# Moving part of one query tile's feed-forward work out of the tail, five instead of six shared head groups before it, and a later due slot for side work

## The chip, the cores and the metric

One NeuronCore of a Trainium2 chip runs one transformer block. The metric is the time of one execution in device microseconds (us). TensorE is called PE here, VectorE is DVE, ScalarE is ACT. "The trace" is the record that the hardware profiler makes of one execution.

Before the change the kernel took 922.74 us (median of 3 runs, 921.8 to 923.44).

## The reference, cut

```python
def _A_ref(x, wqkv, wo):            # B, S, D = 1, 2048, 512; H = 32 heads of 16
    qkv = (x @ wqkv).reshape(B, S, 3, H, Dh).transpose(2, 0, 3, 1, 4)
    scores = jnp.einsum('bhqd,bhkd->bhqk', q, k) * Dh ** (-0.5)
    p = _softmax(scores, axis=-1)
    o = jnp.einsum('bhqk,bhkd->bhqd', p, v)
    return o.transpose(0, 2, 1, 3).reshape(B, S, D) @ wo

def _B_ref(x, w_gate, w_up, w_down):        # F = 1792
    return _gelu(x @ w_gate) * (x @ w_up) @ w_down

h = _layernorm(x) * (1 + ca) + sa           # sa .. gb: six rows of silu(c) @ w_mod
x = x + ga * _A_ref(h, A_wqkv, A_wo)
h = _layernorm(x) * (1 + cb) + sb
x = x + gb * _B_ref(h, B_w_gate, B_w_up, B_w_down)
```

The softmax has 32 x 2048 x 2048 exponentials. On 128 partitions that is 2048 slices of 512 columns.

## The kernel before: the parts that matter

The 2048 queries are worked off in six sets. The last two are single tiles of 128 queries; I call them A (tile 14) and B (tile 15). Heads come in eight "quads" of four heads. For the first six quads, A and B run as one unit of 256 queries; for the last two quads each runs alone, A first.

```python
SETS = ((0, 512), (512, 512), (1024, 512), (1536, 256), (1792, 128), (1920, 128))
QS = 6              # quads in which A and B share a unit
LATE = 48
...
units += [((4, 5), qd, SETS[4][0], 2 * P) for qd in range(QS)]
units += [((k,), qd) + SETS[k] for k in (4, 5) for qd in range(QS, 8)]
```

A "slot" is one slice of 512 score columns. ACT exponentiates most of them, two or three slots in one instruction. Where DVE has room, one slot of three is given to DVE instead, which needs five instructions for it.

Beside the attention of one set, PE works off "side work" of the sets before: output projection, LayerNorm, and the feed-forward block (gate, up, down), all through one PSUM bank. Each piece has a start slot and a due slot, and is spread evenly between them:

```python
due = (ends[1] + 30, ends[2] + 30, ends[3] + 30, n - LATE)    # feed-forward of sets 0..3
...                                                           # then, for A (k):
w.append((lambda: self.near_end(k, 6, self.mi[:, 0:P]), s0, s0))      # normalisers of its
w.append((lambda: self.near_end(k, 7, self.mi[:, 0:P]), s0, s0))      # last two quads
w.append((lambda: self.side_wo(k), s0, s0))                           # output projection
w.append((self.scale_wo, s0, s0))
w.append((lambda: self.near_end(k + 1, 6, self.mi[:, 0:P]), s0, s0))  # B's quad 6
```

What is left when the last exponential is done is the tail. It interleaves A's feed-forward block (14 blocks of 128 hidden columns in four chunks of 4, 4, 4 and 2: 112 gate and up matmuls and 14 down matmuls) with B's whole end: last PV round, normaliser of quad 7, output projection, LayerNorm, and the same feed-forward block.

```python
def tail_end(self, k):                       # B
    ...                                      # normaliser of quad 7, output projection into bank
    self.task([lambda: self.ln_stat(tile, bank)] + self.ln2_steps(k, bank), ("ln2", k))
    self.task([("act", lambda: self.act(self.xs[:, tile, :], bank, ACT.Copy))], ("x1", k))
    yield from self.until(("ln2", k))
    for h in range(2):
        pb = self.scp[:, 4 + h, :]
        yield lambda h=h, pb=pb: self.transp(pb, lambda t: self.normed(k, t), 1, h)
        for i in range(2):
            dc = 2 * h + i
            self.modulate("act" if i == 0 else "dve", self.t2T[:, dc, c0:c0 + W], ...)
    yield from self.tail_ffn(k, self.mi[:, :], (4, 5, 0, 1, 2, 3), 4)
```

The softmax here doesn't subtract the row's maximum and nothing guards it: scores larger than these inputs give would overflow.

## Time and profile before

| | before |
|---|---|
| time | 922.74 us |
| span of the profiled execution | 919.5 us, granted PE clock 0.999 |
| ACT busy | 890.8 us (97%) |
| last exponential ends | 892.92 us |
| from there to the end ("the tail") | 26.56 us |

From the page of the kernel before: span and busy times by engine.

```profile
span 919.5 us, 17368 instructions
PE 779.0 (85%) x7222; PEld 259.7 (28%) x7342; DVE 759.8 (83%) x1482; ACT 890.8 (97%) x749; POOL 3.6 (0%) x11
```

The groups of ACT instructions, shapes kept apart, of the kernel before: the columns after the bar are busy time in us and mean ns of one, then idle time just before them and its cause.

```profile
L309 ACT ACTIVATE E<-ps_sc 128x1536 bf16<-128x1536 f32 x510 | 736.4, 1614 | 1.9 <-PE ps_sc L296 1.9
L309 ACT ACTIVATE E<-ps_sc 128x1024 bf16<-128x1024 f32 x182 | 211.3, 1181 | 0.4 <-PE ps_sc L296 0.4
```

ACT waits for scores only 2.3 us in the whole run. A slice less in an instruction is worth 1614 - 1181 = 433 ns.

The chain that ended last, the kernel before, from the last exponentials on (start, length, what; steps called `issue`, 0.05 us or less, are left out here and below):

```profile
879.47 13.43 ACT E L309 x10
892.92 1.28 ACT L309
...
895.22 0.34 DVE wreg L321
895.56 0.88 DVE rb L333
896.46 0.30 DVE onorm L313
896.81 3.52 PE ps_sc L296 x57
...
914.78 0.70 DVE xw L313
...
916.76 0.42 DVE xs L313
```

Read it from the top. The last exponential ends, ACT loads the table for gelu (1.28 us), DVE modulates tile A (`wreg`) and only then takes the reciprocal of B's last normaliser (`rb`) and normalises (`onorm`). Then PE has B's last output projection, and matmuls almost without a break until the first output step (`xw`) at 914.78 us.

### The profile page before, as it was taken

To read this page: it belongs to the slowest core of one execution; us is meant where nothing else is said; L and a number is where in the kernel's file an instruction comes from. 1 tells how busy PE (TensorE), PEld (TensorE's weight loads), DVE (VectorE), ACT (ScalarE), POOL (GpSimd) and SP (SyncE) were. 2 spreads that over 40 slices of the span, in tenths; PEclk is the share of its full clock that TensorE was granted. 3 is DMA by queue.
4 is the path that set the end of the run, shared out by engine and by line. 5 is a ranking of instruction groups with operands and counts; after the bars stand their busy time and mean duration, and the time that the engine had idled before them with its cause. 6 is when DMAs were issued, how large, how long until landed. Compare 5 with 4: busy or idle time off the path is not lost.

```text
span 919.5 us, 17368 instructions
## 1 busy us (share of the span) xinstructions
PE 779.0 (85%) x7222; PEld 259.7 (28%) x7342; DVE 759.8 (83%) x1482; ACT 890.8 (97%) x749; POOL 3.6 (0%) x11
## 2 busy tenths in 40 slices
PE   8888888878888888888888888888888889988878
PEld 3332222222222222222222222222233223334346
DVE  8756999989897899998896999999998664588764
ACT  6999999999999999999999999999999999999992
POOL 1000000000000000000000000000000000000000
PEclk9999999999999999999999999999999999999999
DMA  9013220000000000000000000000010000000000
GB/s 298 1 24 109 86 89 10 13 14 14 14 13 13 2 13 13 14 13 25 16 11 13 13 13 13 14 2 19 26 26 8 14 8 19 25 15 14 15 14 13
DMA packets 30928, 24.96 MB, mean 27 GB/s; under 512 B 15849, under 2 KB 25634, under 8 KB 30850
## 3 DMA queue, kind: packets, MB, share of 16 engines
q1 hardware_dynamic: 28466, 22.28, 8.2%
q10 hardware_dynamic: 2384, 1.57, 0.6%
q8 instruction: 57, 0.93, 0.4%
q14 instruction: 21, 0.17, 0.1%
HBM read 21.23 MB, written 2.61 MB: 26 GB/s over the span
## 4 chain that ended last, share of the span: by engine, by line
ACT 89%; PE 6%; DVE 3%; issue 0%; DMA 0%; DVEq 0%
ACT E L309 87%; PE ps_sc L296 3%; PE ps_mi L296 2%; ACT wreg L309 2%; PE ps_pv L296 1%; DVE du L326 0%; DVE st L349 0%; DMA xs<-in_A_x_dram 0%; DVE xw L313 0%; DVE nwt L313 0%; DVE dt L321 0%; ACT hreg L309 0%; DVE hreg L321 0%; DVE wreg L326 0%; ACT L309 0%
## 5 line engine op out<-in xcount | busy, mean ns | idle before, releaser
L309 ACT ACTIVATE E<-ps_sc 128x1536 bf16<-128x1536 f32 (+2 forms) x700 | 865.2, 1489 | 12.9 <-PE ps_sc L296 12.9
L296 PE MATMUL ps_sc<-qT,kme 32*128 32x512 bf16 (+2 forms) x1344 | 155.8, 331 | 32.4 <-ACT E L309 23.8
L296 PE MATMUL ps_pv<-E,vaug 128*17 128x512 bf16 (+2 forms) x2439 | 180.1, 329 | 3.3 <-DVE vaug L330 1.1
L296 PE MATMUL ps_sc<-qT,kmo 32*128 32x512 bf16 (+2 forms) x1344 | 154.1, 331 | 31.1 <-ACT E L309 26.4
L321 DVE TENSOR_SCALAR dt<-ps_sc 128x512 int32<-128x512 f32 x154 | 106.4, 691 | 46.2 <-PE ps_sc L296 44.1
L296 PE MATMUL ps_sc<-xs,ident 128*128 128x512 bf16 x264 | 85.7, 384 | 47.0 <-ACT E L309 45.1
L296 PE MATMUL ps_mi<-wreg,mreg 128*128 128x512 bf16 (+1 forms) x421 | 113.9, 355 | 11.8 <-DVE wreg L326 4.5
L326 DVE SCALAR_TENSOR_TENSOR ED<-du,dt 128x512 int16<-128x512 f32 x154 | 104.9, 684 | 0.6
L326 DVE SCALAR_TENSOR_TENSOR du<-du,dt 128x512 f32<-128x512 f32 x154 | 104.2, 682 | 0.3
L326 DVE SCALAR_TENSOR_TENSOR du<-dt 128x512 f32<-128x512 uint16 x154 | 104.1, 683 | 0.2
L296 PEld LDWEIGHTS ps_sc<-qT,kme 32*128 32x128 bf16 x1344 | 41.7, 91 | 137.0 <-ACT E L309 92.2
L296 PEld LDWEIGHTS ps_sc<-qT,kmo 32*128 32x128 bf16 x1344 | 41.2, 91 | 134.5 <-ACT E L309 91.0
L296 PEld LDWEIGHTS ps_pv<-E,vaug 128*17 128x17 bf16 x2439 | 47.7, 88 | 101.4 <-issue 90.6
L321 DVE TENSOR_SCALAR dt<-dt 128x512 f32<-128x512 int32 x154 | 63.8, 417 | 0.5
L296 PE MATMUL ps_pv<-ED,vaug 128*17 128x512 bf16 (+2 forms) x185 | 58.3, 347 | 0.3 <-DVE ED L326 0.2
L296 PE MATMUL ps_mi<-dreg,hreg 128*128 128x512 bf16 x185 | 56.5, 384 | 2.4 <-issue 1.3
L296 PEld LDWEIGHTS ps_mi<-wreg,mreg 128*128 128x128 bf16 x448 | 35.5, 97 | 75.1 <-issue 35.0
L330 DVE CAST wreg<-ps_mi 128x512 bf16<-128x512 f32 x49 | 33.7, 688 | 21.4 <-PE ps_mi L296 20.9
L296 PEld LDWEIGHTS ps_sc<-xs,ident 128*128 128x128 bf16 x293 | 19.7, 97 | 93.2 <-ACT E L309 91.5
L326 DVE SCALAR_TENSOR_TENSOR wreg<-wreg,ps_mi 128x512 bf16<-128x512 bf16 x49 | 33.5, 684 | 10.5 <-PE ps_mi L296 10.1
L296 PE MATMUL ps_mi<-hreg,wreg 128*128 128x512 bf16 x105 | 34.0, 385 | 2.5 <-DVE qT L321 0.9
L313 DVE TENSOR_TENSOR wreg<-wreg 128x1024 bf16<-128x1024 bf16 (+1 forms) x56 | 34.7, 619 | 0.5
(118 smaller groups left out, 505.1 us busy)
## 6 DMA issues: line engine op xcount, KB each, us to landing
rb<-scr_rec SPq DMA_DIRECT2D x96, 64.0 KB, 2.0
mreg<-in_w_mod_dram SPq DMA_DIRECT2D x1, 2048.0 KB, 14.4
out_dram<-xs SPq DMA_DIRECT2D x16, 128.0 KB, 1.7
mreg<-in_B_w_gate_dram SPq DMA_DIRECT2D x4, 448.0 KB, 3.7
mreg<-in_B_w_up_dram SPq DMA_DIRECT2D x4, 448.0 KB, 5.3
rb<-scr_rec SPq DMA_DIRECT2D x56, 32.0 KB, 1.9
dreg<-in_B_w_down_dram SPq DMA_DIRECT2D x3, 512.0 KB, 5.4
wreg<-in_A_wqkv_dram SPq DMA_DIRECT2D x3, 384.0 KB, 10.6
```

The lines of the kernel that those rows point to most:

```text
L296: return self.rec("pe", lambda e: e.matmul(out, lhsT, rhs, start=start, stop=stop, tile_position=tp), [lhsT, rhs], [out], cost=(n, int(rhs ...
L309: return self.rec("act", lambda e: e.activation(out, in_, func, scale=scale, **kw), rd, wr, cost=self.cost("act", out, [in_], "act"))
L313: return self.rec(eng, lambda e: e.tensor_tensor(out, a, b, op), [a, b], [out], cost=self.cost(eng, out, [a, b], "tt"))
L321: return self.rec(eng, lambda e: e.tensor_scalar(out, a, s1, s2, **kw), rd, [out], cost=self.cost(eng, out, [a], "ts"))
L326: return self.rec("dve", lambda e: e.scalar_tensor_tensor(out, a, s, b, op0=op0, op1=op1), rd, [out], cost=self.cost("dve", out, [a, b], " ...
L330: return self.rec(eng, lambda e: e.tensor_copy(out, in_), [in_], [out], cost=self.cost(eng, out, [in_], "ts"))
```

## The change

The intent: with five shared quads, A is finished 48 slots before the end instead of 32. That leaves time to do A's transposes, their modulation and the gate and up projections of its first two chunks (64 of 112 matmuls) beside the last attention, where A's LayerNorm already was. Three settings move as well: the due slot of the feed-forward block of set 2 (`ends[3] + 30` becomes `ends[3] + LAG`, 60); that of set 3, which stays tied to A's end and so comes 16 slots earlier; and the scaling of `wo` for B on DVE, which now waits for A's LayerNorm.

```diff
-QS = 6
+QS = 5
-LATE = 48
+LAG = 60
+EARLY = 2
...
-                       for qd in range(8)], "wo")
+                       for qd in range(8)], "wo", self.after([("ln2", len(SETS) - 2)]))
...
-        nch = len(chunks)
+        nch = len(chunks) if part is None else part
         for ci in range(nch + 1):
             if ci < nch:
                 yield from G(ci)
             if ci >= 1:
                 yield from U(ci - 1)
+        if part is not None:
+            self.done(("part", gi))
+            return
...
-        due = (ends[1] + 30, ends[2] + 30, ends[3] + 30, n - LATE)
+        due = (ends[1] + 30, ends[2] + 30, ends[3] + LAG, ends[-2] - 16)
...
         w.append((self.scale_wo, s0, s0))
+        w.append((lambda: self.side_ffn(k, EARLY), s0, n - 20))
         w.append((lambda: self.near_end(k + 1, 6, self.mi[:, 0:P]), s0, s0))
...
     def tail(self, ka, kb):
+        self.require([("part", ka)])
...
-        yield from self.until(("ln2", k))          # tail_ffn: A's transposes and
-        if k < len(SETS) - 1:                      # modulation leave the tail
-            ...
+        first = EARLY if k < len(SETS) - 1 else 0
+        for ci in range(first):
+            for fc in chunks[ci]:
+                yield lambda fc=fc: self.down_mm(down, c0 // P, fc)
-        for ci in range(len(chunks) + 1):
+        for ci in range(first, len(chunks) + 1):
```

The early chunks use tanh for gelu, the tail the gelu table, as before.

More of the change, by code (lines that the diff above doesn't have):

```diff
@@ L864, in side_wo, with side_ffn @@
             self.task(self.ln2_steps(gi), ("ln2", gi), self.after([("st2", t) for t in tiles]))
-    def side_ffn(self, gi):
+    def side_ffn(self, gi, part=None):
         q0, W = SETS[gi]
@@ L1361, in tail_ffn @@
         c0, tile, kpb = BCOL[k], q0 // P, 512 // W
-        yield from self.until(("ln2", k))
-        if k < len(SETS) - 1:
-            for h in range(2):
-                pb = self.scp[:, banks[h], :]
-                yield lambda h=h, pb=pb: self.transp(pb, lambda t: self.normed(k, t), 1, h)
-                for i in range(2):
-                    dc = 2 * h + i
-                    self.modulate("act" if i == 0 else "dve", self.t2T[:, dc, c0:c0 + W],
-                                  pb.bitcast(BF16)[:, W * i:W * i + W], self.modB, dc)
         chunks = [range(a, min(NFC, a + kpb)) for a in range(0, NFC, kpb)]
@@ L1394, in tail_ffn @@
                     g.rearrange("p (k n) -> p k n", k=n), ALU.mult, ALU.mult)], ("p", k, ci))
-            if ci >= 1:
+            if ci > first:
                 yield from self.until(("p", k, ci - 1))
```

## The prediction

> **What bounds the kernel now.** Until 892.9 us it is ScalarE: the page has ACT busy 890.8 of 919.5 us, and in the groups its exponentials wait for matmuls only 2.3 us. They run back to back (timeline: 13 of 128x1536 in 17.76 us, 1.37 us each). From 892.92 us, the end of the last exponential, to 919.5 us is a tail of 26.6 us: table load, last PV, normaliser and output projection of the last query tile (B), its LayerNorm, then both tiles' gate, up and down projections. In the chain of waits PE holds the tail almost without a break from 896.8 to 914.8 us, then four DVE steps (to 917.2) and the output DMA.
>
> **What changes, by the instruction order of the two programs.**
> - Removed from the tail: 64 of 224 gate/up matmuls (16 took 0.89 us in the chain: 3.6 us), 4 transposes, 2 of 8 gelus and products, tile A's 4 modulations. Two of those held DVE for 0.69 us, so that the reciprocal of B's last normaliser began at 895.48 although its matmul had ended at 894.24.
> - Added beside the attention: the same matmuls, 2 DVE gelu chains (about 2.8 us each), 2 tanhs on ScalarE (0.52 us each in the flow: one began at 839.82, the next exponential at 840.34). DVE is busy only 9.3 of 17 us from 876 to 893, PE 12.8, so both have room; the tanhs cost ScalarE +1.04 us.
> - Moved: 157 instead of 154 DVE exponentials, so three 512-column slices leave ScalarE (0.43 us each, the difference of the means 1614 and 1181 ns): -1.28 us. Quad 5 runs as two 128-query units; a three-slice score group takes 0.39 us as 6 matmuls and 0.40 as 12. Its second DMA round trip (9 to 11 us) starts about 13 us before the end.
> The attention should end at 892.9 - 0.2 us, plus up to 1 us of waits.
>
> The Trainium skill, "ScalarE: Activation LUTs", section "Table sets: the hidden batching unit", puts exp and tanh in one set, so the early tanhs need no load; the trace agrees (2 loads in all, though 28 tanhs lie between exponentials).
>
> **The tail after, from the last exponential's end T.** In the new PE order the last PV waits behind the normaliser matmul of quad 6, which waits for DVE's second up product: I allow 0.3 to 0.7 us. But quad 7's reciprocal starts as soon as its matmul is done. Last output-projection matmul: T+3.4 (before T+3.9). B's LayerNorm has one gelu product before it instead of two: its normalised row is ready at T+8.3 (before T+9.3). A's remaining 48 gate/up matmuls (2.7 us) and 14 downs (3 us) fit into B's waits. Then B alone: transposes, modulation, 112 gate/up matmuls (6.3 us), 14 downs (3 us, the last 2 after a product), two DVE steps: T+20.1, against T+24.3 before, where A's last downs and two DVE steps came after B's. Saving about 4.1 us, nearly all critical, since the tail is one chain.
>
> **Prediction.** 922.7 - 4 = 918.8 us, range 917.0 to 921.0. Faster by over 2%: 0.01, within 2%: 0.98, slower: 0.01.
>
> **Right if** the stretch from the last exponential to the end is 22 to 23 us; that exponential ends within 1 us of 892.7; A's output leaves several us before B's; the groups show 507 and 185 exponentials, under 4 us of waits.
>
> **Wrong if** exponentials wait for PE because the earlier deadlines of the large feed-forward blocks crowd it; if quad 5's normalising, waiting for its DMA, holds DVE just before the end and delays the last PV; or if a tanh waits on DVE. Each would show as ScalarE or DVE idle between 860 and 896 us and could eat 1 to 3 us.

## More of the kernel before

The program is laid out ahead of time, on the host, and whether DVE gets a slot depends on its backlog and on the side work that is owed:

```python
if (('v', 3, 0) in self.have and len(active) < NACT and sum(v >= 4 * rp for v in vec) < 3
        and self.backlog() < BACK and self.free["dve"] < t + 700
        and len(mem) == CH and slack > -100 and self.credit < 1024):
    g = pos + CH * LEAD             # about here, a slot will be DVE's
    ...
```

The recorder inserts all semaphore waits itself, and it keeps any two engines off one PSUM bank at a time, readers too.

## The result, and the profile after

The changed kernel took 919.87 us (median of 4 runs, 919.08 to 921.02), beside 922.27 us before (4 runs). The ratio is 0.9974, with a 95% interval of 0.9956 to 0.9991: within 2%. All outputs are right. Ratios are the mean time of one kernel's runs over that of the other's of the same rounds, so they are not quite the ratio of the medians. Five more rounds later gave 918.88 us and 0.9959 (0.9945 to 0.9973).

From the page of the changed kernel:

```profile
span 919.3 us, 17768 instructions
PE 806.3 (88%) x7461; PEld 262.4 (29%) x7461; DVE 773.6 (84%) x1512; ACT 890.1 (97%) x747; POOL 3.6 (0%) x11
```

The span is 0.2 us shorter, so this profile seems to deny the 2.4 us that the timing shows. It doesn't, and the reason has to be cleared away first. These are the busy times by stretch of the first 40 us; the number after the last engine is the granted PE clock. First the kernel before:

```profile
0.00:20.00 20.00, 16.35 (x122) 7.19 (x124) 16.21 (x56) 11.52 (x18) 3.34 (x10) 1.00 0.96 311
20.00:40.00 20.00, 17.10 (x151) 6.37 (x150) 16.65 (x51) 20.00 (x19) 0.00 (x0) 1.00 0.08 32
```

Then the changed kernel, whose program is the same there:

```profile
0.00:20.00 20.00, 15.20 (x114) 7.50 (x114) 15.07 (x54) 10.73 (x17) 3.34 (x10) 0.91 0.97 308
20.00:40.00 20.00, 18.70 (x148) 6.86 (x144) 16.50 (x52) 18.58 (x17) 0.00 (x0) 0.83 0.09 35
```

In this execution the clock was halved for 3.4 and 6.8 us early on, and from about the tenth exponential on each came 3.16 us later than before. Not all of that is the clock: 0.46 us was there before the first halving, because a load of `x` landed later (ACT's first work on it began at 6.54 us instead of 6.08). From number 219 to number 572 of ACT's exponential instructions the offset is 3.38 us; why it grows there is not explained. Up to number 572 both programs have the same order. So I count from an exponential that all kernels share (number 500 of ACT's, counted from zero, at 636 to 640 us) to the end of the last one (where the table load begins), and from there to the end of the program. These two lengths don't contain the start.

| | DVE exponentials | exponential 500 to the last | tail | sum |
|---|---|---|---|---|
| before | 154 | 256.44 | 26.56 | 283.00 |
| change, first profile | 157 | 256.14 | 23.30 | 279.44 |
| change, second profile (run "again") | 157 | 256.13 | 23.38 | 279.51 |

The two profiles of the change agree within 0.08 us. The change is worth 3.5 us: 0.3 in the attention, 3.2 in the tail.

The same groups and the same chain for the change, first profile:

```profile
L310 ACT ACTIVATE E<-ps_sc 128x1536 bf16<-128x1536 f32 x507 | 732.0, 1603 | 2.1 <-PE ps_sc L297 1.8
L310 ACT ACTIVATE E<-ps_sc 128x1024 bf16<-128x1024 f32 x185 | 214.1, 1175 | 1.1 <-PE ps_sc L297 1.1
```

```profile
894.74 0.70 DVE wreg L327
895.49 0.50 PE ps_mi L297 x2
896.01 0.96 DVE rb L334
896.97 0.16 DVE osb L331
897.17 0.49 PE ps_sc L297 x2
...
904.94 0.47 ACT wreg L310
...
905.51 0.35 DVE wreg L322
...
915.58 0.70 DVE xw L314
916.30 0.42 DVE xs L314
```

The last exponential ends at 896.00 us here. Compare the ends: before, two pairs of output steps stood at the end (A's after B's); now there is one. Two places in this chain become experiments below. The second up product (`wreg` at 894.74) and the normaliser of B's quad 6 (`ps_mi`, `rb` at 896.01) now stand between the last exponentials and the copy of B's last sums (`osb`). And in the modulation of B, ACT comes first (904.94) and DVE after it (905.51). DVE's timeline of the change shows the waits behind them, in brackets:

```profile
894.48 0.29 DVE L314 TENSOR_TENSOR onorm<-osb,rb 128x128 bf16<-128x128 f32 x1 [1.18 <-DMA rb<-scr_rec]
900.77 0.70 DVE L350 BATCH_NORM_STATS2 st<-ps_sc 128x6 f32<-128x512 f32 x1 [1.79 <-ACT xs L310]
905.51 0.69 DVE L322 TENSOR_SCALAR wreg<-ps_sc,modB 128x128 bf16<-128x128 bf16 x2 [0.61 <-ACT wreg L310]
```

### The profile page after: what moved, and what is told of

Read it like the earlier page. It is cut to its first block, busy times and chain, and to the rows that moved or that the text cites. A ratio compares the mean times of both kernels' runs of the same rounds, so it can differ in the third digit from the quotient of the medians.

```text
span 919.3 us, 17768 instructions
## 1 busy us (share of the span) xinstructions
PE 806.3 (88%) x7461; PEld 262.4 (29%) x7461; DVE 773.6 (84%) x1512; ACT 890.1 (97%) x747; POOL 3.6 (0%) x11
## 4 chain that ended last, share of the span: by engine, by line
ACT 87%; PE 6%; DVE 5%; DMA 1%; SPq 0%; issue 0%; DVEq 0%
ACT E L310 84%; PE ps_sc L297 3%; ACT wreg L310 2%; PE ps_mi L297 1%; PE ps_pv L297 1%; DVE du L327 1%; DMA scr_rec<-rden 1%; DVE st L350 0%; DVE dt L322 0%; DMA rb<-scr_rec 0%; SPq L360 0%; DVE xw L314 0%; DVE nwt L314 0%; DVE hreg L322 0%; PE ps_mi L301 0%
## 5 line engine op out<-in xcount | busy, mean ns | idle before, releaser
L322 DVE TENSOR_SCALAR dt<-ps_sc 128x512 int32<-128x512 f32 x157 | 108.4, 690 | 45.8 <-PE ps_sc L297 43.8
L297 PE MATMUL ps_mi<-wreg,mreg 128*128 128x512 bf16 (+2 forms) x512 | 127.2, 340 | 11.4 <-DVE wreg L327 7.0
L297 PE MATMUL ps_sc<-xs,ident 128*128 128x512 bf16 x285 | 92.3, 386 | 42.2 <-ACT E L310 40.2
L327 DVE SCALAR_TENSOR_TENSOR ED<-du,dt 128x512 int16<-128x512 f32 x157 | 106.9, 683 | 0.6
L327 DVE SCALAR_TENSOR_TENSOR du<-dt 128x512 f32<-128x512 uint16 x157 | 106.1, 683 | 0.2
L297 PE MATMUL ps_mi<-dreg,hreg 128*128 128x512 bf16 x210 | 65.3, 385 | 1.7 <-DVE xw L314 1.0
L297 PEld LDWEIGHTS ps_mi<-wreg,mreg 128*128 128x128 bf16 x512 | 38.9, 97 | 76.9 <-issue 35.8
L297 PE MATMUL ps_mi<-hreg,wreg 128*128 128x512 bf16 x120 | 39.2, 390 | 1.6 <-DVE qT L322 0.9
L297 PE MATMUL ps_mi<-wo,onorm 128*128 128x512 bf16 x120 | 36.5, 384 | 0.7 <-DVE xw L314 0.7
```

The costliest lines, as they stand in the source:

```text
L297: return self.rec("pe", lambda e: e.matmul(out, lhsT, rhs, start=start, stop=stop, tile_position=tp), [lhsT, rhs], [out], cost=(n, int(rhs ...
L322: return self.rec(eng, lambda e: e.tensor_scalar(out, a, s1, s2, **kw), rd, [out], cost=self.cost(eng, out, [a], "ts"))
L327: return self.rec("dve", lambda e: e.scalar_tensor_tensor(out, a, s, b, op0=op0, op1=op1), rd, [out], cost=self.cost("dve", out, [a, b], " ...
```

## The experiments

The theory: PE's work in the tail is the limit once B's output projection is done, the moved work pays only as far as A's rest doesn't fit into B's waits, and the attention's length follows the number of slices that DVE takes. The rivals are: what is moved out comes off one for one; the later due slot matters little; the tail is a chain of latencies. "Sum" is as above.

| run | DVE exponentials | exponential 500 to the last | tail | sum | time, ratio to before (interval) |
|---|---|---|---|---|---|
| again | 157 | 256.13 | 23.38 | 279.51 | 918.88, 0.9959 (0.9945 to 0.9973) |
| early0 | 157 | 255.04 | 25.91 | 280.95 | 921.36, 0.9984 (0.9969 to 0.9998) |
| early1 | 157 | 255.56 | 24.45 | 280.01 | 920.39, 0.9975 (0.9960 to 0.9989) |
| early3 | 157 | 257.98 | 27.47 | 285.45 | 924.82, 1.0016 (1.0000 to 1.0031) |
| lagonly | 160 | 253.57 | 26.57 | 280.14 | 920.29, 0.9965 (0.9948 to 0.9982) |
| nolag | 152 | 258.46 | 23.43 | 281.89 | 920.70, 0.9979 (0.9959 to 0.9999) |
| modbank | 157 | 256.15 | 23.06 | 279.21 | 918.23, 0.9959 (0.9932 to 0.9986) |
| ne6 | 157 | 256.13 | 23.12 | 279.25 | 917.89, 0.9946 (0.9929 to 0.9964) |
| repair | 157 | 257.07 | 23.18 | (slow clock) | 919.04, 0.9965 (0.9952 to 0.9977) |
| repairbn | 157 | 256.14 | 22.98 | 279.12 | 918.32, 0.9952 (0.9938 to 0.9966) |
| lag100 | 160 | 255.71 | 24.21 | 279.92 | 921.48, 0.9983 (0.9964 to 1.0002) |
| lagrepair | 160 | 253.55 | 26.59 | 280.14 | 919.22, 0.9970 (0.9955 to 0.9986) |

The timings scatter by some 3 us with the granted clock: of 11 runs of the kernel before, those at clock 1.000 took 921.61 and 921.91 us, those at 0.994 took 924.38 and 924.29. The lengths from the traces repeat within 0.1 us (the change's two profiles; its attention of 256.13 to 256.15 us also in modbank, ne6 and repairbn; the tail before, 26.56 to 26.59 us, in lagonly and lagrepair), with one profile for each kernel but the change.

### again: the same kernel once more

> The changed kernel once more, unchanged. In its first profile every exponential up to the 600th, where both programs are still the same, came 3.16 to 3.38 us later than before, because the TensorE clock was halved twice in the first 40 us; after that point the attention was 0.3 us shorter and the tail 3.3 us shorter. If that offset is a matter of the run (theory), the change itself is worth about 3.6 us: a profile without the early halving spans about 915.9 us, and over five rounds the ratio is about 0.996. If the late start belongs to the changed kernel (rival), its runs stay about 2.4 us ahead or less (0.9974) and the halving shows again while the kernel before does not have it.

The profile of this run had no early halving, spanned 916.4 us (expected 915.9), and the ratio was 0.9959. The halving is a matter of the run: all programs here are the same in the first 40 us, and 5 of the 14 profiles have a halving there; the kernel before also had runs at clocks from 0.994 to 1.000. The Trainium skill fits: "TensorE: Matmul & The Clock Gate", section "What's actually happening", calls the activity window free-running and the cold start run-variable, though it speaks of the first warm-up and not of a second halving. So the first 2.4 us fits as the true 3.5 us less such starts: in the runs at clock 0.999 or above of this call, the change took 917.76 and 918.08 us and the kernel before 921.61 to 921.91. (The full offset ends at number 572, not at the 600th that the expectation names.)

### early0, early1, early3: how many chunks go early

```diff
-EARLY = 2
+EARLY = 0        # then 1, then 3
```

> EARLY = 0: five shared quads, tile A's transposes and modulation still beside the attention, but all of its gate and up projections back in the tail. Measure: from the end of the last exponential to the end of the program (before 26.6 us, change 23.3). Theory (tile B's chain is the limit, A's work costs only what doesn't fit into B's waits): about 25 us, clearly more than half of the 3.6 us of moved matmuls hidden. Rival (the tail is bound by PE work, so what is moved out comes off one for one): 23.3 + 3.6 = 26.9 us.

> EARLY = 1: one chunk of four (32 of 112 matmuls, 1.8 us) beside the attention. Theory: 24.0 us of tail, most of the gain of EARLY = 2 already there. Rival (one for one): 25.1 us.

> EARLY = 3: three chunks (96 of 112 matmuls) before the tail begins. Theory (B's chain is the limit already): tail 23.0 to 23.8 us, no gain over EARLY = 2, and perhaps a loss, since the last up chunk now stands before the last normalisers in PE's order. Rival (one for one): 23.3 - 1.8 = 21.5 us.

A chunk of 32 gate and up matmuls is 1.8 us of PE. The first early chunk shortens the tail by 25.91 - 24.45 = 1.46 us, the second by 24.45 - 23.38 = 1.07 us; so neither one for one, nor as much hidden as the theory's figures (25 and 24.0) had it. Part of what is missing is lost at the front: B's last output-projection matmul ended 3.54, 3.74 and 4.13 us after the last exponential with no, one and two early chunks, so the stretch from there to the last matmul shrank by 1.49 and 1.40 us. Each early chunk also lengthens the attention by 0.52 and 0.57 us, which is its tanh on ACT: the two early tanhs began at 887.79 and 890.97 us in the second profile of the change, and the next exponentials at 888.31 and 891.49, 0.52 us later. Net, the first chunk is worth 0.94 us and the second 0.50 us.

The third chunk costs 5.9 us, far more than expected. Two things happen. ACT's timeline of early3 shows the first: the last tanh waits for DVE after the last exponential, and holds up the table load behind it (so this tail, counted from the load, is even 1.9 us too short).

```profile
893.55 1.46 ACT L310 ACTIVATE E<-ps_sc 128x1536 bf16<-128x1536 f32 x1
896.26 0.63 ACT L310 ACTIVATE wreg<-wreg 128x512 bf16<-128x512 bf16 x1 [1.25 <-DVE wreg L314]
896.91 1.28 ACT L310 ACT_TABLE_LOAD   x1
```

PE's timeline and the stretches of early3 show the second. A's rest no longer fills B's waits, PE stands idle, and the clock is granted at 0.54 just when B's 112 matmuls begin:

```profile
903.80 0.60 PE L297 MATMUL ps_pv<-dreg,hreg 128*128 128x512 bf16 x2 [1.42 <-DVE nwx L322]
906.99 0.40 PE L301 MATMUL ps_sc<-ident,du 128*128 128x128 bf16 x4 [2.59 <-DVE du L322]
```

```profile
895.00:907.00 12.00, 7.88 (x74) 4.70 (x75) 8.44 (x24) 3.00 (x6) 0.00 (x0) 1.00 0.04 12
907.00:914.00 7.00, 6.11 (x58) 5.82 (x59) 1.38 (x3) 1.75 (x4) 0.00 (x0) 0.54 0.01 2
```

PE was busy 7.88 of 12 us before it, and 0.69 of the last 3.4 us, with one idle of 2.59 us. The Trainium skill, "TensorE: Matmul & The Clock Gate", section "What's actually happening", has the gate close after at least one idle window of about 3.4 us; here the window was not wholly idle. All four early3 runs had clocks of 0.993 or 0.994, while the kernels ranged up to 1.000, which fits a halving in every one; only one of them was profiled. So in this profile work in B's waits has a use beyond being hidden: it keeps the clock. The same trace divides the 5.9 us roughly: from the true last exponential (895.01 us) to B's normalised row it took 11.93 us instead of the change's 8.66, at full clock; from there to the end 17.44 instead of 14.72, and the 6.8 us of halved clock lie in this part. That is 3.3 us lost before the row and 2.7 after it.

### lagonly, nolag: the due slot alone, and the change without it

```diff
 # lagonly: the kernel before, and
-        due = (ends[1] + 30, ends[2] + 30, ends[3] + 30, n - LATE)
+        due = (ends[1] + 30, ends[2] + 30, ends[3] + 60, n - LATE)
 # nolag: the change, and
-        due = (ends[1] + 30, ends[2] + 30, ends[3] + LAG, ends[-2] - 16)
+        due = (ends[1] + 30, ends[2] + 30, ends[3] + 30, ends[-2] - 16)
```

> The kernel before with one part of the change alone: the third query set's feed-forward block is due 60 slots after the next set's end instead of 30. Six quads stay shared, nothing of tile A is early. Its program has 160 DVE exponentials (before 154, change 157). Measure: from the 500th exponential that both share to the end of the last one (before 256.44 us, change 256.14). Theory (each slice that DVE takes is 0.43 us less on ScalarE): 256.44 - 6 x 0.43 = 253.9 us with an unchanged tail of 26.5 us, so about 2.6 us faster than before, a large part of the whole change. Rival (the later deadline only moves waits; the gain of the change is all in its tail): 256.4 us and the time of before.

> The changed kernel with that deadline put back to 30 slots. Its program has 152 DVE exponentials and two early tanhs. Theory: 256.14 + 5 x 0.43 = 258.3 us from the 500th to the last exponential, tail as in the change (23.4 us), so 2.1 us slower than the change and only about 1.4 us faster than before. Rival: same as the change.

Both came out within 0.35 us of the theory. One number in the kernel before takes 2.87 us off the attention, and leaves the tail as it was. The groups of lagonly:

```profile
L309 ACT ACTIVATE E<-ps_sc 128x1536 bf16<-128x1536 f32 x504 | 728.8, 1614 | 1.7 <-PE ps_sc L296 1.6
L309 ACT ACTIVATE E<-ps_sc 128x1024 bf16<-128x1024 f32 x188 | 218.0, 1181 | 0.4 <-PE ps_sc L296 0.4
```

Six instructions are one slice shorter (510 to 504), at the same mean times: 6 x 433 ns = 2.6 us. Most of the rest is a wait of 0.24 us for scores, at 790.92 us in the kernel before, that lagonly doesn't have. The traces show where DVE's slots come from: between ACT's exponentials number 560 and 619 DVE takes none before and seven in lagonly, and later one fewer. The likely reason is that side work spread over 30 more slots leaves less owed at once, so that the condition shown above is met more often; this is read from the code, and which clause of it decides was not tested.

The four sums make a square: due slot at 30 or 60, restructuring (five quads, early chunks) absent or present.

| | due 30 | due 60 | gain of the due slot |
|---|---|---|---|
| six quads, nothing early | 283.00 (before) | 280.14 (lagonly) | 2.86 |
| five quads, two chunks early | 281.89 (nolag) | 279.51 (change) | 2.38 |
| gain of the restructuring | 1.11 | 0.63 | |

So most of what the change brings is the due slot. The restructuring itself shortens the tail by 3.1 to 3.2 us, and lengthens the attention by 2.0 us (due 30) or 2.6 us (due 60): two tanhs of about half a microsecond, and two or three slices that DVE no longer takes. Early0 splits it once more. It has all of the restructuring but the early chunks, and beside lagonly its tail is 0.66 us shorter and its attention 1.47 us longer (three slices are 1.30 of that). So five quads, with the moves that go with them, lose 0.81 us by themselves, and the two early chunks bring 1.44. The moves among themselves (five quads, A's transposes early, set 3's due slot, the scaling of `wo`) were not separated.

### modbank: one engine per PSUM bank

```diff
-                self.modulate("act" if i == 0 else "dve", ...      # tail_end, tile B
+                self.modulate("act" if h == 0 else "dve", ...
```

> The changed kernel, but in the tail ScalarE modulates both halves of one PSUM bank and DVE both of the other, instead of one half of each bank each. In the change DVE waited for ScalarE's second half (0.61 us idle), and tile B's first gate matmul started 10.0 us after the last exponential, not at the 9.4 us predicted. Theory (two engines reading one bank are kept apart by a wait): B's matmuls start at about 9.5 us and the tail is 0.4 to 0.6 us shorter, 22.9 us. Rival (DVE has other work then, or PE is late anyway): tail unchanged at 23.3 to 23.4 us.

(The 9.4 us named there is the start that went into the predicted sum; the prediction's text gives only the sum.) DVE's wait of 0.61 us is gone, as its timeline in modbank shows:

```profile
901.79 0.60 DVE L322 TENSOR_SCALAR wreg<-ps_sc,modB 128x128 bf16<-128x128 bf16 x2 [0.16 <-PE ps_sc L301]
```

The tail is 0.32 us shorter (0.24 against the change's first profile), less than the theory's 0.4 to 0.6 but more than the rival's nothing: B's matmuls began 9.85 us after the last exponential, not at 9.5. The trace's chain reaches them through ACT's two modulations of one bank, now one after the other (901.67 to 902.49 us); A's last three down matmuls kept PE until 902.40. The kernel waits there on purpose: the Trainium skill, "PSUM — Partial Sum Buffer", section "PSUM bank collisions raise a hardware error", forbids two engines the same bank and partitions at once, readers included. The runs here show only what keeping to it costs.

### ne6: B's quad 6 between the two up chunks

```diff
         for ci in range(nch + 1):
             if ci < nch:
                 yield from G(ci)
+            if part is not None and ci == part:
+                yield from self.near_end(gi + 1, 6, self.mi[:, 0:P])
             if ci >= 1:
                 yield from U(ci - 1)
...
-        w.append((lambda: self.near_end(k + 1, 6, self.mi[:, 0:P]), s0, s0))
```

> The changed kernel with the normaliser of tile B's quad 6 put between the first and the second up chunk of tile A, instead of after both. In the change its reciprocal (0.96 us) stands on DVE ahead of the copy of quad 7's sums, which ends 1.12 to 1.21 us after the last exponential, before the change 0.77. Theory (that order costs 0.4 us on the chain): the copy ends at about 0.8 us, quad 7 is normalised at about 2.6 instead of 3.0 to 3.1, and the tail is 22.9 to 23.0 us. Rival (the last PV or the second up chunk, now in front of it on PE, takes its place): no gain, or a last PV later than 0.43 us after the last exponential.

The copy of quad 7's sums ended 0.96 us after the last exponential (change 1.12 and 1.21), quad 7 was normalised at 2.82 (change 2.98 and 3.08), the tail was 23.12 us. So the order costs about 0.26 us (0.18 against the first profile) and not 0.4: the second up product is now in front of the copy instead.

### repair and repairbn: both together, and the statistics first

repair joins ne6 and modbank. repairbn also holds ACT's copy of B's projection back until DVE has taken the row statistics from the same bank:

```diff
-        self.task([lambda: self.ln_stat(tile, bank)] + self.ln2_steps(k, bank), ("ln2", k))
-        self.task([("act", lambda: self.act(self.xs[:, tile, :], bank, ACT.Copy))], ("x1", k))
+        self.task([lambda: self.ln_stat(tile, bank)], ("st2", tile))
+        self.task(self.ln2_steps(k, bank), ("ln2", k), self.after([("st2", tile)]))
+        self.task([("act", lambda: self.act(self.xs[:, tile, :], bank, ACT.Copy))], ("x1", k),
+                  self.after([("st2", tile)]))
```

> The changed kernel with both repairs of its tail together: the normaliser of tile B's quad 6 between the two up chunks of tile A (0.26 us alone) and one engine per PSUM bank for tile B's modulation (0.32 us alone). If the two lie on the same chain and add up (theory): tail 23.38 - 0.26 - 0.32 = 22.8 us, attention unchanged at 256.13 us from the 500th to the last exponential, ratio to before about 0.9955. If PE's queue of tile A's work hides one of them (rival): 23.05 us.

> As repair, and tile B's row statistics on DVE ahead of ScalarE's copy of the same PSUM bank, which they waited for (0.60 us) before. Theory of the chain (tile B's LayerNorm is what the tail waits for): its normalised row comes 0.6 us earlier, at 7.8 us after the last exponential, and the tail shrinks by as much, to 22.2 us. Rival (after the output projection PE has hardly a gap: about 14.8 us of matmuls stand in the 15.5 us between 4.1 and 19.6 us after the last exponential): the row comes earlier, but the tail shrinks by 0.3 us or less, 22.5 to 22.8 us, and tile A's last downs move behind B's.

repair's profile fell in an execution whose record shows a granted clock of 0.949 almost throughout, so its lengths can't be compared with the others (matmuls of 512 columns in its tail began 224 ns apart at the median, 216 elsewhere), and whether the two repairs add up stays open. Its four other runs were at 0.994 to 0.998.

repairbn decides the larger question, for the rival. The normalised row of B was ready 7.22 us after the last exponential, 1.4 us before the change's 8.66, yet the tail was 22.98 us, 0.40 less than the change's, 0.08 to 0.14 less than with one of the repairs alone, and far from the 22.2 of a latency chain. (It is also above the rival's own 22.5 to 22.8, which started from 22.8 for repair, a figure that was not confirmed.) DVE and PE in repairbn:

```profile
898.54 0.70 DVE L350 BATCH_NORM_STATS2 st<-ps_sc 128x6 f32<-128x512 f32 x1 [1.09 <-PE ps_sc L297]
```

```profile
912.38 1.24 PE L297 MATMUL ps_pv<-dreg,hreg 128*128 128x512 bf16 x5
```

The statistics no longer wait for ACT. But five of A's down matmuls, which used to run before B, are now the last thing on PE. From the output projection on, PE has the same work to do and hardly a gap; which tile goes first changes little. The stretches from the end of B's last output-projection matmul to the last matmul show it (length, then PE busy), in the kernel before, the change (second profile) and repairbn:

```profile
897.20:915.82 18.62, 18.40 (x245) 14.69 (x245) 9.18 (x23) 5.53 (x11) 0.00 (x0) 1.00 0.01 2
897.10:912.61 15.51, 15.03 (x187) 11.38 (x188) 8.02 (x21) 4.56 (x9) 0.00 (x0) 1.00 0.03 10
898.50:913.62 15.12, 14.99 (x191) 11.47 (x188) 7.99 (x21) 4.45 (x9) 0.00 (x0) 1.00 0.01 1
```

So 3.1 of the 3.2 us that the change takes off the tail is this stretch of PE work.

### lag100: a still later due slot

repair, with `LAG = 100` instead of 60.

> As repair, with the deadline of the third query set's feed-forward block at 100 slots instead of 60. Its program has 160 DVE exponentials (repair 157). By the rule of 0.43 us for each slice: 256.13 - 1.28 = 254.85 us from the 500th to the last exponential, tail as in repair, so 1.3 us faster than repair. Rival (the rule fails when side work is pushed up against the last deadline, where ScalarE then waits for PE or DVE): 255.5 us or more, or a tail over 23.3 us, and waits of the exponentials for scores between 800 us and the end.

The program has three more DVE exponentials than repair, but the attention shrank by only 0.43 us instead of 1.28 (256.14 to 255.71; the 256.14 is repairbn's, since repair's own profile had the slower clock), and the tail grew to 24.21 us. In PE's timeline the last up chunk waits for DVE:

```profile
892.20 1.07 PE L297 MATMUL ps_mi<-wreg,mreg 128*128 128x128 bf16 x16 [1.28 <-DVE rb L334]
893.19 0.40 PE L297 MATMUL ps_pv<-E,vaug 128*17 128x128 bf16 x16
```

The last exponential ended at 892.31 us, the last PV round only 1.29 us after it (0.43 in the change). Exponentials also waited: from number 500 on 0.8 us for scores, nearly all of it at 862.32 and 868.19 us, against 0.05 in the change. That is most of the 0.85 us missing from the attention. So the rule of 0.43 us a slice did not hold here, where side work is pushed up against the end.

### lagrepair: the kernel before, its due slot, and the repairs of its tail

> The kernel before with the 60-slot deadline, and with the two repairs that need none of the restructuring (one engine per bank for tile B's modulation, statistics ahead of ScalarE's copy). No tile A work is early, six quads stay shared. lagonly had 253.57 us from the 500th to the last exponential and a tail of 26.57. Theory (that tail is bound by PE, which has all of tile A's and B's gate, up and down matmuls in it): hardly any gain, tail 26.2 to 26.6 us, so the restructuring is needed for a shorter tail. Rival (the tail is a chain of latencies there too): 0.9 us shorter, 25.6 us, and the restructuring is worth nothing over it.

The row of B was ready 0.41 us earlier (8.85 instead of 9.26), and the tail stayed at 26.59 us. This is the theory: that tail has all of A's and B's matmuls in it and is bound by them (from the output projection on PE was busy 18.53 of 18.65 us). To shorten it, work has to leave it.

### A version that beats both?

By the lengths, repairbn has the smallest sum, 279.12 against 279.51 of the change. In the timings that is not to be told: runs at clock 0.999 or above took 917.36 and 918.14 us (repairbn), 917.49 and 917.48 (modbank), 917.55 and 917.56 (ne6) and 917.76 and 918.08 (change), with 921.39 to 921.91 before.

## Why the prediction was right or wrong

The forecast was 918.8 us, in a range of 917.0 to 921.0, and within 2%; 919.87 and later 918.88 were measured. The range held. That 918.88 lies so near the forecast is partly luck: the tail saved 0.9 us less than forecast, and the starts of runs differ by up to 3 us. Point by point:

- **The attention ends 0.2 us earlier: right.** 0.3 us. Three slices left ACT, two tanhs came, and exponentials waited no more than before (2.1 us in the second profile, 2.3 before). But the step was only counted, not explained. I read 157 DVE exponentials off the instruction order and didn't ask which line of the diff made them. The due slot gave six, the restructuring took back three (lagonly, nolag).
- **The tail is 4.1 us shorter: mechanism right, size too large.** It was 3.2 us, 23.3 to 23.4 in all and not "22 to 23". The term "T+20.1" for the end of DVE's last step measured 20.7 and 20.8. Of that, B's last output-projection matmul began at 3.65 and 3.75 instead of 3.4, the normalised row came at 8.56 and 8.66 instead of 8.3, and the rest fell after the row: B's modulation had ACT and DVE one after the other on each bank (modbank: 0.32 us). The last 0.3 us is the output DMA: 2.29 us from DVE's last step to the end before, 2.57 after. It is 2.29 or 2.30 in the three kernels with six shared quads and 2.55 to 2.63 in all with five, so it goes with the program; why, I did not find out.
- **"Nearly all critical, since the tail is one chain": wrong as a reason.** Up to the output projection it is a chain of latencies. From there on it is PE's work (repairbn, lagrepair), a stretch that fell from 18.62 to 15.51 us. The early chunks helped because they took matmuls away, at 1.46 and 1.07 us of tail for 1.8 us of matmuls.
- **"A's remaining matmuls fit into B's waits": right for the change, and it cuts both ways.** One chunk less in those waits (early3), and PE idles there and the clock halves.
- **The last PV behind quad 6's normaliser, "0.3 to 0.7 us": the place was right, the form was not.** The PV round itself ended 0.43 us after the last exponential, as before. The 0.35 to 0.44 us came one step later: quad 6's reciprocal stood before the copy of quad 7's sums.
- **Quad 5's DMA holding DVE: it happened, and cost little.** DVE idled 1.18 us for it. The up matmuls that the next step needs anyway ended about 0.2 us before that step could start, so I put the cost at 0.2 us; this is read from the timeline, not tested.
- **A's output leaves several us before B's: right.** A's last output step ended 11.3 us after the last exponential, B's 20.7.
- **No table load for the early tanhs: right.** Two loads before and after, as the Trainium skill's "ScalarE: Activation LUTs", section "Table sets: the hidden batching unit", has it for functions of one set.

## What to carry to other kernels

When a change to a scheduled kernel moves several settings, count what each of them does to the instructions of the bounding engine, and run them apart: here one due slot brought 2.4 to 2.9 of the 3.5 us, and the rebuilt tail 0.6 to 1.1. Moving work out of a tail pays only the part that its waits don't already hide, less what it costs beside the main work, and work left in those waits can keep the PE clock up (one profile here, early3). To compare profiles by fractions of a microsecond, measure from an instruction that both programs share, since the start of a run can differ by 3 us.

## What the Trainium skill lacked or had wrong

- "TensorE: Matmul & The Clock Gate" gives a warm-up of about 3.4 us and a closing of the gate after an idle window. It gives no figure for windows that are only partly idle. Here the clock was halved after 3.4 us stretches with PE busy 1.85 and 2.20 us (first profile of the change, from 10.8 and 21.1 us on) and 0.69 us (early3), the longest idle in them being 1.55, 1.08 and 2.59 us.
- The same page says that the granted share is half or full and never between (13/16 apart, as a limit for several cores). One profiled run of one core here (repair) has 0.949 on record for 901 us, and its 512-column matmuls were 224 ns apart instead of 216.
- "ScalarE: Activation LUTs" puts a switch of tables at 1283 ns of load and about 1380 ns of drain. The load agrees (1.28 us), but no drain shows here: the load began at 892.92 us, with the end of the last exponential, and the next activation at 894.21.
